# Identity products in TensorE's planned waits: a fused linear attention and SiLU layer on one core

## The chip, the cores and the metric

The kernel runs on one core of a Trainium2 chip. The metric is device time of one execution in microseconds (us), the median of several runs. The profile is one further execution, recorded by the hardware profiler; its times are told from the start of its span, and a line such as L830 is a line of the kernel's code.

## The reference

Two stages follow each other. The first is a block-wise linear attention with decay over 4 batches, 8 heads, 768 positions and 64 features per head; the second is a layer of 512 to 2048 to 512 features with SiLU between, over the 3072 tokens that the first yields.

```python
for b in range(nb):                      # blocks of 64 positions
    intra = einsum('bhic,bhjc->bhij', qb, kb) * Dmask
    intra = einsum('bhij,bhjd->bhid', intra, vb)
    inter = einsum('bhid,bhde->bhie', qb * lam_pow, kv_state)
    out[:, :, sl] = intra + inter
    kv_state = lam_block * kv_state + einsum('bhsd,bhse->bhde', kb * rev_pow, vb)
x = out.transpose(0, 2, 1, 3).reshape(B * S, H * D)
h = x @ w_in
return (h * sigmoid(h)) @ w_out
```

## The kernel before

The work is cut into units of 128 positions of one batch, 24 of them. Twelve sets of two units each carry the attention; the first four sets are the first 256 positions of one batch each ("paired", L414 to L556), the others are the same 128 positions of two batches.

Of a set, k, q and v are loaded by SyncE's queue (L349 for the first four sets, L351 after), 512 KB each. VectorE or ScalarE casts k and q to bf16 (`kq`, through the helper `copy`, L313 and L315). TensorE turns them with the identity into `tr` (L442), and they are copied back as `kqT`. VectorE scales v into `vd` (L320, the helper `tt`, where all its additions and products are recorded). TensorE then makes the state products `d_ps` (L463), the scores `st_ps` (L514), and, when VectorE has masked the scores, the outputs `x_ps` (L538 from the block itself, L543 from the carried state). VectorE makes the carried state of `d_ps` (the tiles `y`, `xf`), and ScalarE or GpSimd copies it into `xe` (L317 is GpSimd's copy). VectorE brings `x_ps` out as `xt`.

The layer's first product (`product1`, L830) takes 128 features of w_in at a time as the stationary operand; for the first four groups of units a quarter of w_in serves 16 products of 128x256, in two banks of PSUM. ScalarE applies SiLU (L839) into `g`. The second product is plain for the first eight units (L861, a bank per unit, four products to each quarter of w_out) and by a seven-product scheme of Strassen's kind for the others (L1072); the last group's first product uses such a scheme too (L944).

The weights are loaded and cast to bf16 by GpSimd's queue in quarters: L364 for w_in, L367 for w_out. Their order among the sets' loads is a string, `SEQUENCE = "s0 i0 s1 i1 i2 s2 i3 o0 s3 o1 o2 o3 s4"`. Where weights follow a set in it, GpSimd first copies one column of that set's k (`gate`, L331), so it waits for that load to land; all these GpSimd tasks stand in a chain (`prior`), and its copies of `xe` stand in the same instruction stream.

All other order comes from the class `Planner`. Each piece of work is a task with a key (its priority), the engines that may run it with a cost for each, the tasks that it depends on, and the buffers that it needs from pools of fixed size (8 banks of PSUM under "bank"). `order()` runs an event loop over planned time: at each event, an engine that is free takes the ready task of the lowest key whose buffers can be had; a buffer comes back to the end of its pool when the last task that uses it has its planned end; a task takes slots from the front. Loads are modelled as shares of the DMA engines. The list that comes out is the order in which the kernel then emits its instructions, on each engine, and each engine runs its own in that order. So planned times decide the order and the slots, and on the chip semaphores make each instruction wait for its data. TensorE may start at a planned 0.8 us (`BEGIN`).

The identity that the turns use is a constant, `ident` (L252 to L257), made by GpSimd early on.

Of the kernel before, what the change touches and what calls it, by code (L numbers as in the profile page):

```python
# [8 lines left out]
F32 = mybir.dt.float32  # L9
# [28 lines left out]
class Planner:  # L38

    LAT = {"PE": 0.23, "ACT": 0.06, "DVE": 0.06, "POOL": 0.08, "SP": 0.0}  # L40
    BEGIN = {"PE": 0.8, "ACT": 8.3, "DVE": 4.5, "POOL": 4.7, "SP": 0.8}
    FIRST, LAST, AHEAD = {"SP": 1.9, "ACT": 1.15, "POOL": 2.5}, 1.0, 0.75

    def __init__(self, pools):
        self.pools = {n: list(range(c)) for n, c in pools.items()}
        self.tasks = []

    def add(self, key, on, fn, deps=(), bufs=(), nbytes=0, kind=None, prior=(), late=0.0):
        key = key if isinstance(key, tuple) else (key,)
        t = Task(key, on, fn, deps, list(bufs) + [b.with_ for b in bufs if b.with_], nbytes, kind, prior, late)  # L50
        for b in t.bufs:
            b.left += 1
        self.tasks.append(t)
        return t

    def order(self):
        for i, t in enumerate(self.tasks):
            t.key = (t.key, i)
            t.left = len(t.deps) + len(t.prior)
            for d in t.deps:  # L60
                d.users.append(t)
            for d in t.prior:
                d.next.append(t)
        free = dict(self.BEGIN)
        waiting = {e: [] for e in free}
        ready = {e: [] for e in free}
        events, release, out = [], [], []
        started = set()
        queues = {e: [] for e in ("SP", "POOL", "ACT")}
        clock = [0.0]  # L70
        seq = 0

        def arm(t):
            for e in t.on:
                heapq.heappush(waiting[e], (t.ready, t.key, id(t), t))
            heapq.heappush(events, t.ready)

        def finish(t, e):
            nonlocal seq
            for b in t.bufs:  # L80
                b.left -= 1
                if not b.left:
                    seq += 1
                    heapq.heappush(release, (t.end, seq, b))
                    heapq.heappush(events, t.end)
            for u in t.users:
                u.left -= 1
                u.ready = max(u.ready, free[e] if e == "PE" and "PE" in u.on else t.end)
                if not u.left:
                    arm(u)  # L90

        def transfer(now):

            while True:
                at = clock[0]
                active = [(e, q[0]) for e, q in queues.items() if q and q[0][1] <= at + 1e-9]
                later = [q[0][1] for q in queues.values() if q and q[0][1] > at + 1e-9]
                cycle = max([sum(j[3][1] for _, j in active)] + [j[3][2] for _, j in active])
                speed = [16e-3 * j[3][0] / cycle for _, j in active]
                step = min([j[2] / v for (_, j), v in zip(active, speed)] + [x - at for x in later], default=None)  # L100
                if step is None or at + step > now + 1e-9:
                    if now > at:
                        for (_, j), v in zip(active, speed):
                            j[2] -= (now - at) * v
                        clock[0] = now
                    return None if step is None else at + step
                clock[0] = at + step
                for (e, j), v in zip(active, speed):
                    j[2] -= step * v
                    if j[2] <= 1e-9:  # L110
                        queues[e].pop(0)
                        j[0].end = clock[0] + self.LAST + j[0].late
                        finish(j[0], e)

        events += free.values()
        heapq.heapify(events)
        for t in self.tasks:
            if not t.left:
                arm(t)
        while len(out) < len(self.tasks):  # L120
            if not events:
                stuck = [t for t in self.tasks if id(t) not in started and not t.left]
                raise RuntimeError(f"plan stuck after {len(out)} of {len(self.tasks)}: "
                                   f"{[(t.key, list(t.on), [b.pool for b in t.bufs]) for t in stuck[:8]]}")
            now = heapq.heappop(events)
            after = transfer(now)
            while release and release[0][0] <= now:
                _, _, b = heapq.heappop(release)
                self.pools[b.pool].append(b.slot)
            for e in free:  # L130
                while waiting[e] and waiting[e][0][0] <= now:
                    _, key, i, t = heapq.heappop(waiting[e])
                    heapq.heappush(ready[e], (key, i, t))
                if free[e] > now:
                    continue
                if e == "SP" and sum(j[2] for j in queues[e]) > self.AHEAD:
                    continue
                kept, took, short = [], None, set()
                while ready[e]:
                    key, i, t = heapq.heappop(ready[e])  # L140
                    if i in started:
                        continue
                    need = {}
                    for b in t.bufs:
                        if b.slot is None:
                            need[b.pool] = need.get(b.pool, 0) + 1
                    lacks = {p for p, n in need.items() if len(self.pools[p]) < n}
                    if lacks or short & set(need):
                        short |= lacks
                        kept.append((key, i, t))  # L150
                        continue
                    mine = now + t.on[e]
                    if any(max(free[o], now) + d < mine - 1e-9 for o, d in t.on.items() if o != e):
                        kept.append((key, i, t))
                        continue
                    took = t
                    break
                for k in kept:
                    heapq.heappush(ready[e], k)
                if took is None:  # L160
                    continue
                t = took
                started.add(id(t))
                for b in t.bufs:
                    if b.slot is None:
                        b.slot = self.pools[b.pool].pop(0)
                free[e] = now + t.on[e]
                heapq.heappush(events, free[e])
                out.append((now, len(out), e, t))
                for u in t.next:  # L170
                    u.left -= 1
                    u.ready = max(u.ready, free[e])
                    if not u.left:
                        arm(u)
                if t.nbytes:
                    start = max(free[e] + self.FIRST[e], queues[e][-1][1] if queues[e] else 0.0)
                    queues[e].append([t, start, t.nbytes, t.kind])
                    after = transfer(now)
                else:
                    t.end = free[e] + self.LAT[e]  # L180
                    finish(t, e)
            if after is not None:
                heapq.heappush(events, max(after, now + 1e-6))
        transfer(now + 100.0)
        return out
# [3 lines left out]
def kernel(  # L189
# [10 lines left out]
    nc = tc.nc  # L200
# [29 lines left out]
    plan = Planner(POOLS)  # L230
    add = plan.add

    def tile_of(b, shape, dt, name):
        if b.tile is None:
            pool = ps if b.pool == "bank" else sb
            b.tile = pool.tile(shape, dt, tag=f"{b.pool}{b.slot}", name=name)
        return b.tile
# [4 lines left out]
        out=lam_sb,  # L242
# [7 lines left out]
    for t in xe_tiles:  # L250
        nc.vector.memset(t, 0.0)
    ident = const.tile([128, 128], BF16, name="ident")  # L252
    nc.gpsimd.memset(ident, 0.0)
    nc.gpsimd.affine_select(
        out=ident, in_=ident, compare_op=AL.not_equal, fill=1.0,
# [9 lines left out]
    for c, r in enumerate(halves):  # L265
        nc.gpsimd.affine_select(
            out=tri[r], in_=tri[r], compare_op=AL.is_ge, fill=0.0,
# [6 lines left out]
    for r in halves:  # L274
        nc.gpsimd.iota(iota_2[r], pattern=[[0, 1]], base=0, channel_multiplier=2)
        for a in range(2):
            for b in range(2):
                nc.gpsimd.affine_select(
                    out=tri_2[r, a, b], in_=tri_2[r, a, b], compare_op=AL.is_ge, fill=0.0,
# [511 lines left out]
    for si, o in enumerate(infos):  # L791
# [6 lines left out]
        else:  # L798
            if open_ is None:
                after_first(o, burst((o.s - 0.5, 0), [first_part(o)]))  # L800
            else:
                a, b = second_part(open_), first_part(o)
                t = burst((o.s - 0.5, 0), [a, b])
# [334 lines left out]
    for i in range(PLAIN, NU, 4):  # L1138
        product2(by_rank[i:i + 4])

    for _, _, e, t in plan.order():
        t.fn(e)

# [29 lines left out]
```

## Time and profile before

| What | Value |
|---|---|
| three runs | 206.91, 207.32, 209.9 us; median 207.32 |
| the profiled execution's own time | 207.82 us |
| its span, first to last instruction | 206.1 us |
| mean granted TensorE clock over the span | 0.989 |
| busy: TensorE, weight loads, VectorE, ScalarE, GpSimd | 187.0, 132.9, 134.8, 107.4, 52.4 us |
| moved by DMA | 33.92 MB, mean 165 GB/s |
| TensorE busy from 0 to 20 us | 9.66 us |
| TensorE busy from 20 to 25 us | 1.66 us |
| TensorE busy from 25 to 60 us | 34.79 us |

How to read it: the busy time of TensorE (PE) is that of overlapping matmuls whose ends are modelled, so it tells where the engine stood still rather than how well it ran. The granted clock is the share of full speed that the throttle let through. The chain that ended last is followed back from the last instruction, at each step to what released it; its shares say which engine's work made up the span. A landing is the time from a load's issue to its last byte.

### The profile page before, as it was taken

What the parts mean: (1) busy time and instruction counts of PE and PEld (TensorE: products, weight loads), DVE (VectorE), ACT (ScalarE), POOL (GpSimd) and SP (SyncE); (2) the same over time, 40 slices, a digit from 0 to 9 for tenths busy, and PEclk for the clock granted to TensorE, in tenths of its full rate; (3) what the DMA queues carried; (4) which work ended last, traced back from release to release, by engine and by line L of the source; (5) the groups of instructions that cost most, each with busy time, mean ns of one, the idle gap of its engine ahead of it and who ended that gap; (6) DMA issues with size and microseconds to landing.
All of it is one profiled execution on the core that took longest, in us unless ns stands there. A gap on an engine that the chain in (4) does not pass through costs nothing.

```text
span 206.1 us, 5719 instructions
## 1 busy us (share of the span) xinstructions
PE 187.0 (91%) x2445; PEld 132.9 (64%) x2464; DVE 134.8 (65%) x249; ACT 107.4 (52%) x195; POOL 52.4 (25%) x76
## 2 busy tenths in 40 slices
PE   0459399999999999999999999998999999999993
PEld 0347288786667565544578648474675778888882
DVE  6488632767950467716989953999758995665411
ACT  3637267874336453375734492745615453766420
POOL 7231400401130111222565013346003221222200
PEclk9999889999999999999999999999999999999999
DMA  3999999999999999999999999905101110102213
GB/s 99 292 253 260 228 222 265 235 199 214 228 238 249 156 216 231 238 219 195 263 213 234 203 213 240 244 7 117 39 3 54 51 54 0 54 0 102 88 52 118
DMA packets 88617, 33.92 MB, mean 165 GB/s; under 512 B 67088, under 2 KB 87568, under 8 KB 88592
## 3 DMA queue, kind: packets, MB, share of 16 engines
q1 hardware_dynamic: 79232, 23.60, 57.3%
q0 software_dynamic: 4224, 4.19, 12.2%
q10 hardware_dynamic: 5136, 5.77, 8.7%
q8 instruction: 19, 0.31, 0.7%
q14 instruction: 6, 0.05, 0.1%
HBM read 27.27 MB, written 6.29 MB: 163 GB/s over the span
## 4 chain that ended last, share of the span: by engine, by line
PE 82%; DMA 8%; DVE 7%; issue 1%; ACT 0%; POOL 0%; POOLq 0%; DVEq 0%
PE h_ps L830 31%; PE o_ps L1072 22%; PE o_ps L861 13%; PE h_ps L944 6%; DMA w_in_bf<-in_moe_w_in_dram 5%; DMA raw<-in_k_dram 3%; PE x_ps L687 2%; DVE s L320 2%; PE tr L442 2%; DVE g L320 1%; PE d_ps L647 1%; PE x_ps L679 1%; PE st_ps L657 1%; PE x_ps L538 1%; DVE kq L315 1%
## 5 line engine op out<-in xcount | busy, mean ns | idle before, releaser
L830 PE MATMUL h_ps<-xt,w_in_bf 128*128 128x256 bf16 (+1 forms) x439 | 75.7, 322 | 4.7 <-DMA w_in_bf<-in_moe_w_in_dram 3.3
L839 ACT ACTIVATE g<-h_ps 128x512 bf16<-128x512 f32 x80 | 47.1, 594 | 45.7 <-PE h_ps L830 45.0
L830 PEld LDWEIGHTS <-w_in_bf 128*128 128x128 bf16 x448 | 43.7, 99 | 30.1 <-DMA w_in_bf<-in_moe_w_in_dram 3.5
L861 PE MATMUL o_ps<-w_out_bf,g 128*128 128x512 bf16 x118 | 29.7, 379 | 0.6 <-issue 0.2
L320 POOL TENSOR_TENSOR s<-g,s 128x512 bf16<-128x512 bf16 x16 | 19.0, 1188 | 43.1 <-DVE s L320 26.8
L320 DVE TENSOR_TENSOR st<-st_ps,tri 128x512 bf16<-128x512 f32 x32 | 20.5, 681 | 11.2 <-PE st_ps L657 11.2
L1072 PEld LDWEIGHTS <-g 128*128 128x128 bf16 x256 | 24.9, 98 | 4.4 <-ACT g L839 0.3
L320 DVE TENSOR_TENSOR xt<-x_ps,lam_xe 128x512 bf16<-128x512 f32 x24 | 15.9, 699 | 15.2 <-PE x_ps L687 9.5
L1072 PEld LDWEIGHTS <-s 128*128 128x128 bf16 x192 | 18.7, 98 | 2.6
L861 PEld LDWEIGHTS <-g 128*128 128x128 bf16 x128 | 12.1, 98 | 12.0
L320 POOL TENSOR_TENSOR vd<-raw,lam_v 128x512 bf16<-128x512 f32 x10 | 13.3, 1334 | 25.1 <-DMA raw<-in_v_dram 19.7
L313 ACT ACTIVATE kq<-raw 128x512 bf16<-128x512 f32 x27 | 16.2, 621 | 2.1 <-DMA raw<-in_q_dram 1.6
L320 DVE TENSOR_TENSOR osb<-o_ps,m 128x512 f32<-128x512 f32 (+1 forms) x15 | 8.7, 583 | 10.9 <-ACT m L313 6.8
L1072 PE MATMUL o_ps<-wsum,g 128*128 128x256 bf16 x128 | 15.3, 272 | 0.0
L1072 PE MATMUL o_ps<-w_out_bf,s 128*128 128x256 bf16 x128 | 15.3, 273 | 0.0
L442 PE MATMUL tr<-ident,kq 128*128 128x128 bf16 x64 | 7.0, 260 | 8.8 <-POOL gate L331 6.9
L1072 PE MATMUL o_ps<-w_out_bf,g 128*128 128x256 bf16 x128 | 15.0, 273 | 0.0
L320 DVE TENSOR_TENSOR s<-g 128x512 bf16<-128x512 bf16 x16 | 8.2, 510 | 10.4 <-ACT g L839 6.6
L313 ACT ACTIVATE m<-o_ps 128x512 f32<-128x512 f32 (+1 forms) x14 | 7.0, 503 | 11.4 <-PE o_ps L1072 11.4
L320 DVE TENSOR_TENSOR vd<-raw,lam_v 128x512 bf16<-128x512 f32 x14 | 9.2, 681 | 5.0 <-DMA raw<-in_v_dram 5.0
L313 ACT ACTIVATE osb<-o_ps 128x512 f32<-128x512 f32 (+1 forms) x12 | 6.7, 562 | 10.4 <-PE o_ps L861 6.5
L315 DVE CAST kq<-raw 128x512 bf16<-128x512 f32 x21 | 9.1, 451 | 3.8 <-DMA raw<-in_k_dram 2.0
(88 smaller groups left out, 215.1 us busy)
## 6 DMA issues: line engine op xcount, KB each, us to landing
raw<-in_k_dram SPq DMA_DIRECT2D x12, 512.0 KB, 8.2
raw<-in_q_dram SPq DMA_DIRECT2D x12, 512.0 KB, 8.5
raw<-in_v_dram SPq DMA_DIRECT2D x12, 512.0 KB, 8.0
out_dram<-osb ACTq DMA_DIRECT2D x20, 256.0 KB, 3.6
w_in_bf<-in_moe_w_in_dram POOLq DMA_DIRECT2D x4, 512.0 KB, 10.0
w_out_bf<-in_moe_w_out_dram POOLq DMA_DIRECT2D x4, 512.0 KB, 11.7
out_dram<-osb ACTq DMA_DIRECT2D x4, 128.0 KB, 1.7
out_dram<-osb SPq DMA_DIRECT2D x4, 128.0 KB, 1.7
```

Of the source, the lines that this page charges most:

```text
L313: nc.scalar.activation(o, i, AF.Copy)
L315: nc.vector.tensor_copy(o, i)
L320: (nc.vector if e == "DVE" else nc.gpsimd).tensor_tensor(o, a, b, op=op)
L442: nc.tensor.transpose(t[:, m, a], o.kq_of()[:, i, m, a], ident)
L538: nc.tensor.matmul(t[rh, m], lhsT=o.vd_of()[r, 2 * m + h, a, :], rhs=o.st_of(h)[r, m, a], start=m == 0 and a == 0, stop=True, skip_group_c ...
L647: nc.tensor.matmul(d_of(c)[rp, j, m, :], lhsT=o.kq_of()[r, j, 0, m, p, :], rhs=o.vd_of()[r, j, 2 * m + p, :], start=j == 0 and m == 0, sto ...
L687: nc.tensor.matmul(x_of(c)[:, j, m, :], lhsT=o.xe[c].tile[:, (bs[0] + j) % 2, m, :], rhs=o.kqT_of()[:, j, 1, m, halves[c]], start=False, s ...
L830: nc.tensor.matmul(t[:, j, :], lhsT=w_in_bf[:, ko, 128 * (m1 + j):128 * (m1 + j) + 128], rhs=xt[gi].tile[:, ko, :], start=(ko == 0), stop= ...
L839: nc.scalar.activation(t[:, half * per:half * per + per], bank.tile, AF.Silu)
L861: nc.tensor.matmul(t, lhsT=g.tile[:, j, 128 * gp:128 * gp + 128], rhs=w_out_bf[:, ko, :], start=(ko == 0), stop=(ko == KO - 1))
L944: nc.tensor.matmul(t[:, j, :], lhsT=W[w]()[:, k2, f:f + 128], rhs=X(r)[:, k2, :], start=first and j == 0 and k2 == 0, stop=True, skip_grou ...
L1072: nc.tensor.matmul(t[:, i_, :], lhsT=src(j)[:, k2, 128 * r:128 * r + 128], rhs=W[w]()[:, 2 * j + k2, :], start=first and i_ == 0 and j == ...
```

## The change

The planner gets a filler. In its event loop, where TensorE is free and no task can be started, between a planned 1.7 and 30 us and with more than two banks free, it takes the bank that came back last, books TensorE for 0.44 us (before 6 us) or 0.22 us (after), gives the bank back at the end of that time, and puts the filler into the list. A filler issues four matmuls of the identity with itself, 128x128 each, into the four quarters of the bank. Nothing reads what they write.

```diff
+    WARM, COLD = (1.7, 30.0), 6.0
...
+        self.filler = None
...
-        while len(out) < len(self.tasks):
+        fillers = 0
+        while len(out) < len(self.tasks) + fillers:
...
                 if took is None:
+
+                    if e == "PE" and self.filler and self.WARM[0] <= now < self.WARM[1] and len(self.pools["bank"]) > 2:
+                        b = Buf("bank")
+                        b.slot = self.pools["bank"].pop()
+                        free[e] = now + (0.44 if now < self.COLD else 0.22)
+                        seq += 1
+                        heapq.heappush(release, (free[e], seq, b))
+                        heapq.heappush(events, free[e])
+                        out.append((now, len(out), e, self.filler(b)))
+                        fillers += 1
                     continue
...
+    def filler(b):
+        def go(e):
+            t = tile_of(b, [128, 4, 128], F32, "ones")
+            for i in range(4):
+                nc.tensor.matmul(t[:, i, :], lhsT=ident, rhs=ident, start=i == 0, stop=True, skip_group_check=True)
+
+        return Task("filler", {"PE": 0.22}, go, [], [])
+
+    plan.filler = filler
     for _, _, e, t in plan.order():
         t.fn(e)
```

## The prediction

> **What bounds the kernel now.** I read the page first: its 40 slices and the shares of the chain that ended last.
>
> ```profile
> span 206.1 us, 5719 instructions
> ...
> PE   0459399999999999999999999998999999999993
> ...
> PEclk9999889999999999999999999999999999999999
> DMA  3999999999999999999999999905101110102213
> ...
> PE 82%; DMA 8%; DVE 7%; issue 1%; ACT 0%; POOL 0%; POOLq 0%; DVEq 0%
> ```
>
> TensorE is full from the sixth slice to the last. Its holes are all in the first 24 us, and the granted clock dips in slices five and six, right behind the last hole. The DMA engines are full from the second slice to the 26th (about 134 us), so in that time loads land when bytes allow, not when somebody asks earlier. The waits of TensorE by the view of waits are, from 5 to 30 us, 6.9, 3.3, 1.3, 0.9, 0.9 and 0.2 us; from 30 us on they are this and 0.2 us of issue:
>
> ```profile
> PE h_ps L830 <- DVE xt L320: 0.7, 1, 0.7
> ```
>
> Next the chain in order of time (start, length, what), for the place of the hole:
>
> ```profile
> 9.40 0.94 PE tr L442 x7
> ...
> 13.59 0.12 POOL gate L331
> 13.71 10.23 DMA w_in_bf<-in_moe_w_in_dram
> ...
> 23.99 3.41 PE h_ps L830 x16
> ...
> 28.87 1.75 PE h_ps L830 x16
> ```
>
> The second quarter of w_in is issued at 13.71 and lands at 23.94. The first 16 products on it take 3.41 us, where 16 of the same shape take 1.75 us at 28.87: 1.66 us lost. Busy time by stretch, cut so that each has one clock (columns: length, then busy time and count of PE, PEld, DVE, ACT, POOL, then granted clock, DMA share, GB/s):
>
> ```profile
> 10.57:13.98 3.41, 1.71 (x64) 1.33 (x63) 2.83 (x6) 1.55 (x4) 0.78 (x3) 1.00 1.19 219
> 13.98:17.40 3.42, 3.15 (x50) 2.57 (x51) 3.39 (x8) 1.77 (x4) 1.76 (x3) 1.00 1.15 308
> 17.40:20.81 3.41, 3.03 (x85) 2.38 (x82) 2.43 (x6) 2.60 (x6) 0.00 (x0) 1.00 1.21 237
> 20.81:24.22 3.41, 0.23 (x3) 0.21 (x3) 3.11 (x6) 1.45 (x3) 2.15 (x5) 1.00 1.19 217
> 24.22:27.64 3.42, 3.42 (x28) 2.26 (x29) 0.00 (x0) 1.10 (x3) 0.26 (x1) 0.50 1.18 242
> ```
>
> After a stretch with 0.23 us of work the clock is 0.50 for 3.42 us. The column shows 1.00 before 17.4 too, but the durations there are those of a halved clock: eight transposes take 0.94 us at 7.28 and 9.40, and 0.45 us at 28.42. So TensorE is slow until about 17.4, fast, and slow once more from 24.22 to 27.64.
>
> Last, what stands behind that loss: loads that TensorE meets just after they land.
>
> ```profile
> 28.70 1.47 PE L830 MATMUL h_ps<-xt,w_in_bf 128*128 128x256 bf16 x12
> ...
> 37.10 0.45 PE L463 MATMUL d_ps<-vd,kq 64*64 64x64 bf16 x32
> ...
> 51.36 3.62 PE L861 MATMUL o_ps<-w_out_bf,g 128*128 128x512 bf16 x15
> ```
> ```profile
> 35.24 1.29 DVE L320 TENSOR_TENSOR vd<-raw,lam_v 128x512 bf16<-128x512 f32 x2 [3.72 <-DMA raw<-in_v_dram]
> ```
> ```profile
> DMA to landing us min/median/max: 7.8/10.0/13.2
> ```
> ```profile
> DMA to landing us min/median/max: 8.0/11.7/13.3
> ```
>
> The third quarter of w_in (issued 14.46, 13.2 us to land, the first of the two landing lines) is there at 27.7 and first used at 28.70: 1.0 us of slack. VectorE waits 3.72 us for the third set's v, starts its two products at the landing (35.24) and ends at 36.53; the state products that need them start at 37.10: 0.57 us of slack. The last quarter of w_out (third of the issues that start at 37.40, so 38.9, plus 13.3) lands at 52.1; TensorE comes to it after eight products of 0.216 us from 51.36, at 53.09: 1.0 us of slack.
>
> **The change part by part.** It takes nothing away. It adds fillers: wherever the planner finds TensorE with nothing to start between 1.7 and 30 us of its own time, it books 0.44 us (0.22 from 6 us on) and a free bank, and issues four 128x128 products of the identity.
>
> How many: the planner's own list for the unchanged code, gone through by hand of its rules, leaves TensorE unoccupied for 5.6 us up to the first transposes, then 1.6, 2.1, 2.6, 0.9, 1.7 and 0.5 us. That is 10 + 5 fillers before the first transposes, then 7 + 9 + 12 + 4 + 8 + 2 = 42, 57 in all, 228 products. From the trace alone: 12 us idle between 1.7 and 30 give about 45.
>
> What one takes: four products of the transposes' shape, by their rows 0.45/8 x 4 = 0.225 us at full clock and 0.94/8 x 4 = 0.47 us at half. So the booked 0.22 fits the full clock only.
>
> (a) The first 15 start once the identity is made (GpSimd's select on it ends at 1.37) and fill up to between 6.5 us (clock up after 3.4 us) and 1.4 + 15 x 0.47 = 8.5 us (never up). The transposes' data is ready at 7.24. I take their start at 7.4 and the clock up by then, since 3.15 us of work in 3.42 brought it up at 17.4: -0.49 us for the transposes, +0.15 for the fillers. Bounds: -0.5 to +1.2 us.
>
> (b) The next 16 hold TensorE until about 9.4 and 11.8 us, near where the real products start now (9.40, 12.04). The v of the first set lands at about 10.0 by its median of 8.0 us from 1.93, so VectorE's two products (1.28 us, now at 10.70) can start 0.5 us sooner and the states at 11.8. GpSimd's copy at 13.14, its gate at 13.59 and the load at 13.71 hang on that chain. Queued behind the copy on GpSimd are both the second and the third quarter of w_in. I take 0.3 us sooner (bounds 0.7 sooner, 0.5 later), so w_in's second quarter at 23.6.
>
> (c) The 12 that follow the scores run to about 15.5; the transposes that now run from 14.02 to 15.47 are queued behind them, and the x products (now 15.39) wait for VectorE's masks until about 15.2. Late by 0.3 to 0.5 us, repaid by 0.46 us from the transposes and 0.5 us from the x products at full clock: nothing net. With the clock still halved this cover is gone, and it costs 12 x 0.25 = 3.0 us.
>
> (d) The 8 in the hole at 20.65 take 1.8 us. Each writes a bank that VectorE must have read (its copy ends at 20.77), so they start there and end at about 22.6, a microsecond short of the load. The stretch then holds 1.8 + 0.4 us of work in place of 0.23. The nearest rows: 0.23 of 3.41 lost the clock, 3.03 of 3.41 kept it; 1.71 of 3.41 did not win it. Unknown between; I take kept (2.2 is nearer to 3.03 than to 0.23). Worth 1.66 us if kept, 0 if not.
>
> (e) The last two, 0.45 us, stand ahead of the third quarter's products. With (b) and (d), TensorE would come to these at 28.70 - 0.3 - 1.66 + 0.45 = 27.2 and the load lands at 27.4: 1.3 us sooner than now.
>
> (f) What is late next: the states at 37.10 would be reached at 35.8, and v still lands at 35.2, because the DMA engines are full. The second half waits for VectorE until 36.6, so they end near 36.85 in place of 37.5: 0.6 us is left of 1.3. The w_out quarter's 1.0 us of slack then covers it, and later waits are nothing. PSUM: a filler takes a bank only where more than two are free, so a real task loses at most one filler's 0.22 us, counted above.
>
> Sum against the profiled execution (207.82 us, span 206.1): 207.82 - 0.6 = 207.2. The three runs have their median 0.5 us below it, 207.32, so 206.7 for the median.
>
> [...]
>
> **The rivals.**
> No gain reaches the end: the clock is lost in (d) all the same, or the median run had not lost it, or the fillers of (a) and (c) give back what it saves. For it: slack of only 0.57 us at 37.10, 0.5 us between the profiled execution and the median. Against: 1.66 us is three times that slack. 207.1 to 208.3 us; centre 207.4.
> All of it reaches the end: the DMA order shifts so that v and the w_out quarters land sooner as well. For it: half of w_in is issued sooner. Against: DMA share 1.15 to 1.21 throughout, nothing idle to use. 1.66 + 0.3 gives 205.4, bounds 204.8 to 206.2.
> Slower: identity products do not raise the clock. Then 40 fillers up to 24 us take 0.25 us more than booked, 10 us; the hole takes 1.5 of it, so TensorE comes to the second quarter 8 us late: about 215. From 17 such fillers (17 x 0.25 = 4.2 us) it decides the sign past the bound. Against: the transposes, also against the identity, were part of the 3.15 us that raised it at 17.4.
> The plan comes out in another order: fillers shift planned starts by up to 0.2 us, and choices between ScalarE and VectorE follow. A microsecond or two either way; the 0.7 us wait at 140.6 on VectorE shows one place where it would count.
>
> **How the numbers follow.** Forecast (206.2 to 207.1) 0.55; no gain 0.22; all of it 0.12; another order, 205 to 209, 0.06; slower 0.05. The predicted time is the first's, 206.7. The range 205.4 to 208.4 takes in the first two, half of the third, and most of the fourth. Two per cent, 4.1 us, is about what a measurement of this kernel can tell from no change: past it lies the slower rival, 0.05, and on the fast side hardly anything, 0.02, since the whole loss at the clock is 1.66 us. Within it 0.93.
>
> **What would show it.** Right: about 225 more products with the identity before 30 us; eight transposes in 0.45 us from the first set on; 16 products in 1.75 us behind w_in's second quarter and no 0.50 in the clock between 20 and 30 us; then a new wait of TensorE on VectorE's vd near 36, and v landing at 35 as before. Wrong: transposes starting past 8 us (a), the gate's load issued later than 13.7 (b), x products past 16 us (c), the clock at 0.50 again (d), or no new wait at 36 and a time below 206 (f).

## The result and the profile after

The changed kernel takes 218.09 us (median of 6, 217.69 to 218.24) against 207.27 us for the kernel before beside it; the ratio of the mean times is 1.050, with a 95% interval from 1.0445 to 1.0551. A few executions take longer (of the kernel before up to 215.0 us, and one of booked_right 333 us), and they stand outside the ratios and the counts below. The forecast was 206.7 us, with 0.05 on a kernel slower by over 2%. The profiled execution took 218.16 us, 10.3 us more than that of before.

From the page of the changed kernel, the same rows as those shown of before:

```profile
span 216.4 us, 6181 instructions
...
PE   6998999999999999999999999998999999999993
...
PEclk9999999999999999999999999999999999999999
DMA  3999999999913999999999999890601110102213
...
PE 91%; DVE 5%; issue 2%; ACT 0%; POOL 0%; POOLq 0%; DVEq 0%
```

The holes of TensorE are filled and the clock's dip is gone, as the change says. But the whole span is 10 us longer, and the DMA engines, full before, now have a hole of their own in slices 12 and 13. TensorE's waits (us in total, times, longest), all that the view of waits lists:

```profile
PE ones L1158 <- POOL ident L267: 1.4, 1, 1.4
PE h_ps L843 <- DVE xt L333: 0.7, 1, 0.7
PE o_ps L874 <- issue: 0.2, 1, 0.2
```

No wait on another engine has taken the place of the old ones: from 1.44 us on, TensorE hardly waits for any of them. So the 10 us are in what stands in its own queue. The chain in order of time (start, length, what) shows it:

```profile
2.10 0.60 PE ones L1158 x4
2.74 0.60 PE ones L1158 x4
...
10.42 0.58 PE ones L1158 x4
11.00 0.85 PE tr L455 x8
...
15.81 0.40 PE ones L1158 x4
16.20 0.04 issue
16.25 0.40 PE ones L1158 x4
...
19.71 0.40 PE d_ps L476 x30
```

`ones` is a filler's tile. Fillers start 0.64 us apart at half clock and 0.44 us apart at full clock; the plan booked 0.44 and 0.22. Of the 0.44, the four products begin within 0.17 us, the last needs 0.22 us more to its end, and 0.04 to 0.06 us pass before the next filler begins. Between eight transposes there is no such stop. TensorE's weight loads, which the view of waits lists apart, show the stops as waits of about 0.2 us each, 9.6 us in 50 of them:

```profile
PEld L1158 <- issue: 9.6, 50, 0.2
```

What is waited for stands in the trace's semaphores (the counters by which one instruction tells another that it is done). 50 of the 58 fillers follow another filler directly. The first product of each of these waits for a semaphore that TensorE alone raises, and the instruction that raised it last is the last product of the filler before.

The first transposes, whose data is there at 7.3 us, start at 10.8 in place of 6.95 (by the timeline), and the first state products at 19.6 in place of 11.4. GpSimd's gate and the loads of w_in's second and third quarters hang on these (timeline of GpSimd after):

```profile
21.23 0.18 POOL L344 COPY gate<-raw 128x1 f32<-128x1 f32 x1
21.35 1.50 POOL L377 DMA_DIRECT2D w_in_bf<-in_moe_w_in_dram  x2
```

The loads start at 21.35, 7.6 us later than the 13.71 of before.

The sum over the whole of TensorE: there are 58 fillers (the forecast said 57), and the time from the start of each of their products to the next start on TensorE adds up to 27.7 us; they were booked 10 x 0.44 + 48 x 0.22 = 15.0 us. They filled 13.5 us of waits of before. The fillers and the first wait of 1.4 us, less the old waits, are 27.7 + 1.4 - 13.5 = 15.6 us, and 10.3 came out at the end. The other 5.3 us was saved by the real work: its products, counted in the same way and without the waits, take 182.6 us in place of 187.8, since less of them runs at half clock (the 16 products behind w_in's second quarter: 1.75 us in place of 3.41).

### The profile page after: what moved, and what is told of

Its sections match the earlier page's. It is cut to its first block, busy times and chain, and to the rows that moved or that the text cites. A ratio compares the mean times of both kernels' runs of the same rounds, so it can differ in the third digit from the quotient of the medians.

```text
span 216.4 us, 6181 instructions
## 1 busy us (share of the span) xinstructions
PE 206.5 (95%) x2677; PEld 148.3 (69%) x2696; DVE 132.8 (61%) x247; ACT 107.9 (50%) x195; POOL 51.6 (24%) x78
## 4 chain that ended last, share of the span: by engine, by line
PE 91%; DVE 5%; issue 2%; ACT 0%; POOL 0%; POOLq 0%; DVEq 0%
PE h_ps L843 30%; PE o_ps L1085 21%; PE o_ps L874 13%; PE ones L1158 12%; PE h_ps L957 6%; PE x_ps L700 2%; PE tr L455 2%; DVE s L333 2%; DVE g L333 1%; PE d_ps L660 1%; PE x_ps L551 1%; PE x_ps L692 1%; PE st_ps L670 1%; PE d_ps L476 1%; DVE y L333 1%
## 5 line engine op out<-in xcount | busy, mean ns | idle before, releaser
L843 PE MATMUL h_ps<-xt,w_in_bf 128*128 128x256 bf16 (+1 forms) x439 | 74.7, 317 | 1.2 <-DVE xt L333 0.7
L843 PEld LDWEIGHTS <-w_in_bf 128*128 128x128 bf16 x448 | 43.0, 98 | 25.8 <-DVE xt L333 1.0
L1158 PE MATMUL ones<-ident 128*128 128x128 bf16 x232 | 26.1, 245 | 4.5 <-POOL ident L267 1.4
L1158 PEld LDWEIGHTS <-ident 128*128 128x128 bf16 x232 | 18.3, 110 | 11.5 <-issue 9.6
L333 POOL TENSOR_TENSOR vd<-raw,lam_v 128x512 bf16<-128x512 f32 x10 | 11.4, 1140 | 25.9 <-DMA raw<-in_v_dram 25.8
L326 ACT ACTIVATE kq<-raw 128x512 bf16<-128x512 f32 x28 | 17.0, 621 | 0.5 <-DVE osb L333 0.4
L326 ACT ACTIVATE kqT<-tr 128x512 bf16<-128x512 bf16 x8 | 4.6, 589 | 12.5 <-DVE kqT L328 7.2
```

The costliest lines, as they stand in the source:

```text
L326: nc.scalar.activation(o, i, AF.Copy)
L333: (nc.vector if e == "DVE" else nc.gpsimd).tensor_tensor(o, a, b, op=op)
L843: nc.tensor.matmul(t[:, j, :], lhsT=w_in_bf[:, ko, 128 * (m1 + j):128 * (m1 + j) + 128], rhs=xt[gi].tile[:, ko, :], start=(ko == 0), stop= ...
L1158: nc.tensor.matmul(t[:, i, :], lhsT=ident, rhs=ident, start=i == 0, stop=True, skip_group_check=True)
```

## The experiments

Three theories stood at first. W: a filler that takes a bank writes a new tile there, so it waits until the products of the filler before, in the same bank, have come to their end (have drained). M: four products of that kind take that long by themselves. O: the planner's order of tasks, which the booked fillers change, costs the time. Times are medians; ratios are of mean times to the kernel before on the same chip, with 95% intervals. The name behind each heading is that of the run.

**The plan without the products** (plan_only).

```diff
 def go(e):
-    t = tile_of(b, [128, 4, 128], F32, "ones")
-    for i in range(4):
-        nc.tensor.matmul(t[:, i, :], lhsT=ident, rhs=ident, ...)
+    pass
```

> The planner books all 58 fillers as in the change, but nothing is issued for them: the order and the slots are those of the change, the products are left out. Theory W (each filler waits until the products of the one before have drained, because it writes the same bank as a new tile, so it takes 0.64 us at half clock and 0.44 us at full clock where 0.44 and 0.22 are booked): the time of before, 206.5 to 208. Theory M (four such products with their weight loads take that long by themselves): the same, 206.5 to 208. Theory O (the other order of tasks and the other banks cost the time): 214 or more.

Measured: 208.1 us, ratio 1.0044 (1.0017 to 1.007). The order is not where the 5% are: O falls as their cause. A cost of 0.4% is left, which lies with the order and the slots or what follows from them; the interval, 0.2 to 0.7%, excludes that it is nothing.

**The same tile again** (one_tile).

```diff
+    ones = {}
...
 def tile_of(b, shape, dt, name):
     if b.tile is None:
         pool = ps if b.pool == "bank" else sb
+        if name == "ones" and b.slot in ones:
+            b.tile = ones[b.slot]
+            return b.tile
         b.tile = pool.tile(shape, dt, tag=f"{b.pool}{b.slot}", name=name)
+        if b.pool == "bank":
+            ones.pop(b.slot, None)
+            if name == "ones":
+                ones[b.slot] = b.tile
     return b.tile
```

> All 58 fillers are issued, but a filler that takes a bank whose last user was a filler writes the same tile again, so it needs no wait for itself. Theory W: a filler takes 0.43 us at half clock and 0.22 us at full clock, the first transposes start between 7.2 and 8.0 us, the load of w_in's second quarter is issued near 13.7, time 206 to 208. Theory M: fillers stay at 0.64 and 0.44 us and the time at 217 to 219. Theory O: 214 or more. The part of the prediction on the clock: no stretch at half clock between 20 and 30 us, 206.7.

Measured: 208.69 us, ratio 1.0082 (1.0046 to 1.0119). All 232 products are still there. Timeline of TensorE:

```profile
1.44 5.60 PE L1166 MATMUL ones<-ident 128*128 128x128 bf16 x60 [1.44 <-POOL ident L275]
6.99 0.90 PE L463 MATMUL tr<-ident,kq 128*128 128x128 bf16 x8
...
12.96 2.62 PE L1166 MATMUL ones<-ident 128*128 128x128 bf16 x44
...
25.42 0.64 PE L559 MATMUL x_ps<-st,vd 64*64 64x128 bf16 x31
27.17 0.21 PE L559 MATMUL x_ps<-st,vd 64*64 64x128 bf16 x1 [1.11 <-issue]
```

Eleven fillers (44 products) take 2.62 us with the drain of the last, 0.22 us each; in the change they were 0.44. The transposes start at 6.99 and the second quarter's load at 13.63. The 50 waits of the weight loads in the change are down to one:

```profile
PEld L1166 <- issue: 0.5, 1, 0.5
```

M falls: the same products without the wait cost what was booked. Taking the wait away brings back some nine of the eleven us. The time misses W's range all the same: 1.4 us over the kernel before are left, which W did not expect. In the profiled execution 1.1 us of idle time stands in the last line of the timeline above, a stop of TensorE that the last section comes back to.

**Twice the waits** (split).

```diff
-t = tile_of(b, [128, 4, 128], F32, "ones")
-for i in range(4):
+for h in range(2):
+    c = Buf("bank")
+    c.slot = b.slot
+    t = tile_of(c, [128, 4, 128], F32, "ones")
+    for i in (2 * h, 2 * h + 1):
         ...
```

> As the change, but each filler's four products go to two tiles of the same bank, two each, so there are twice as many waits for the filler's own products and as many products as before. Theory W: 0.33 x 2 = 0.66 us for a filler at full clock and 0.48 x 2 = 0.96 at half, so 58 fillers take 13 to 17 us more than in the change: 229 to 236. Theory M (the products themselves take the time): 218.

Measured, in two executions: 239.59 us, ratio 1.155 (1.1479 to 1.1613). M's 218 us is excluded. The direction is W's, but the time is past its range: the chain of this run has the half fillers 0.43 us apart far past the place where the clock rose in the change.

```profile
16.61 0.39 PE ones L1161 x2
16.99 0.04 issue
17.04 0.39 PE ones L1161 x2
```

That is 0.85 us for a filler, where W had 0.66 us at full clock: two products in each 0.43 us did not bring the clock up, and its first rise in the trace is at 50.5 us. The miss is in the clock, not in the wait.

**Booked as long as they take** (booked_right).

```diff
-    WARM, COLD = (1.7, 30.0), 6.0
+    WARM, COLD = (1.7, 30.0), 14.0
...
-                        free[e] = now + (0.44 if now < self.COLD else 0.22)
+                        free[e] = now + (0.64 if now < self.COLD else 0.44)
```

> The fillers keep their tiles and their waits, but the planner books 0.64 us before a planned 14 us and 0.44 us after, so there are 27 of them. Theories W and M: TensorE comes to its real work about as in the plan, first transposes near 8 us, 206.5 to 208.5. Theory O, in which fillers do harm by moving the order: 212 or more. A fourth way, that any product of the identity slows the loads by its reads: 212 or more as well, with a lower rate of DMA.

Measured: 207.6 us, ratio 1.0012 (0.9984 to 1.0041). With its waits left in, a filler does no harm when the plan knows its length: there are then 27, which end when the real work comes due (first transposes at 7.01). This run has half as many products as the change, so by itself it does not show that the products do nothing to the loads; one_tile, with all 232 of them, does to within its 1.4 us. Together they put the loss down to the waits, times their number, in a queue that runs in order.

**Only ahead of the first transposes** (early_only).

```diff
-    WARM, COLD = (1.7, 30.0), 6.0
+    WARM, COLD = (1.7, 6.0), 6.0
```

> Fillers only up to a planned 6 us: 10 of them, with their tiles and waits. Theories W and M: 10 x 0.64 = 6.4 us from 1.44, so the first transposes start at 7.9 in place of 7.28, and w_in's second quarter is issued 0.3 to 0.7 us later than 13.71; 207.3 to 208.5. Theory O: 212 or more, since the booked time already moves the order. If the fillers raise the clock before the transposes, these take 0.45 us and the delay is repaid: 207.0.

Measured: 209.25 us, ratio 1.0085 (1.0054 to 1.0116), somewhat above the range of W. The ten fillers take 6.4 us and the transposes start at 7.60, 0.65 us late, at half clock (eight in 0.9 us): ten fillers with waits do not raise it. The load of w_in's second quarter starts at 14.16, 0.45 us late, as expected. The trace has two further waits of TensorE on VectorE, of 0.6 and 0.8 us near 105 and 111 us, that before does not have; whether they come of the order or of the delay was not told apart.

**One wide product in place of four** (wide_one). It starts from one_tile; the order in which the tiles `xe` are set to zero is turned round, so that the one that the fillers read is there first.

```diff
-t = tile_of(b, [128, 4, 128], F32, "ones")
-for i in range(4):
-    nc.tensor.matmul(t[:, i, :], lhsT=ident, rhs=ident, ...)
+t = tile_of(b, [128, 512], F32, "ones")
+nc.tensor.matmul(t, lhsT=ident, rhs=xe_tiles[-1][:, 0].rearrange("p m e -> p (m e)"), ...)
...
-    for t in xe_tiles:
+    for t in xe_tiles[::-1]:
```

> As one_tile, but a filler is one product of the identity with 512 columns of zeros in place of four of 128 columns: the same 0.22 and 0.43 us, a quarter of the instructions. It asks what is left of one_tile's 1.4 us over the kernel before. Theory F: in one_tile TensorE stood still for 1.3 us at 25.84 with nothing to wait for, at its 961st instruction, 512 instructions after a like stop in booked_right and 2048 ahead of one in plan_only, because its code had not been fetched; with 348 instructions fewer the stop goes or is short, and the time is 206.3 to 207.6. Theory O: the planner's other order costs it; the time is that of plan_only, 207.8 to 208.5.

Measured: 207.62 us, ratio 1.0008 (0.9975 to 1.0041). The median is just past F's range and under O's, and the stop on issue is gone from the trace (0.2 us, as in the change, is all that is left under that name). The interval lies under one_tile's, but the trace has new short waits on ScalarE (1.1 us) in the stop's place, and one execution cannot tell how often the stop comes. So F's time fits, nearly, and its cause is not shown (last section).

**Only the hole in front of w_in's second quarter** (hole_only), the part of the prediction that carried its gain; the tile is kept as in the second experiment.

```diff
-    WARM, COLD = (1.7, 30.0), 6.0
+    WARM, COLD = (20.0, 24.0), 6.0
```

> Fillers without the wait for themselves (one_tile's way) only between a planned 20 and 24 us: nine of them, and the order of all tasks is that of the kernel before. It tests the sum of the prediction by itself. If the clock is kept and the loads' slack lets 0.6 us through: ratio 0.997. If an execution of the kernel before mostly doesn't lose the clock there, or the loads give it all back: ratio 0.999 to 1.002. If the clock falls all the same: 1.000 with a stretch of half clock in the profile.

Measured: 207.02 us, ratio 0.9972 (0.9946 to 0.9998). Busy time by stretch (columns as in the prediction), then the timeline of TensorE:

```profile
20.81:24.22 3.41, 2.25 (x46) 2.02 (x35) 3.38 (x7) 1.46 (x3) 2.04 (x4) 1.00 1.19 217
24.22:27.64 3.42, 3.10 (x60) 2.48 (x58) 1.08 (x3) 1.75 (x4) 0.40 (x1) 1.00 1.18 251
```
```profile
21.12 1.95 PE L1166 MATMUL ones<-ident 128*128 128x128 bf16 x32 [0.17 <-DVE y L341]
24.06 1.92 PE L851 MATMUL h_ps<-xt,w_in_bf 128*128 128x256 bf16 x16 [0.99 <-DMA w_in_bf<-in_moe_w_in_dram]
...
36.19 0.32 PE L484 MATMUL d_ps<-vd,kq 64*64 64x64 bf16 x16
36.69 0.32 PE L484 MATMUL d_ps<-vd,kq 64*64 64x64 bf16 x16 [0.18 <-DVE vd L341]
```

With 2.25 us of busy time in 3.41 the clock is kept, the 16 products behind the load take 1.9 us with the end of the last, and TensorE comes to the state products at 36.2 and waits there for vd, where before it came at 37.1 and did not wait.

**Two variants of it**, one with the wide product (hole_wide) and one with the change's own fillers and their waits (hole_waits).

> As hole_only, but each of the nine fillers is one product of the identity with 512 columns of zeros: 18 instructions in place of 72. It is the best guess from the runs so far, and a second test that the work in the hole is worth something. If what it does is to keep the clock: ratio 0.995 to 0.999, like hole_only's 0.9972. If hole_only's gain was chance: 0.999 to 1.002. If zeros do not count as work for the clock: a stretch of half clock behind the hole, 1.000.

Measured: 207.17 us, ratio 0.9985 (0.996 to 1.001).

> The change's own fillers, with their waits, only between a planned 20 and 24 us: nine of them. Theory W: 0.44 us each, so one delays the state products by 0.2 us and eight take 3.5 us from 20.8 on, up to 24.3, 0.3 us past the landing of w_in's second quarter. The clock is kept or not by products that fill about half of each 0.44 us; in the change it stayed at full with them. Kept: ratio 0.997 to 1.001. Lost: 1.001 to 1.004. Theory M gives no other time here.

Measured: 207.41 us, ratio 0.9996 (0.9971 to 1.0021). Its eight fillers run from 21.9 to 25.2 with full clock after them (the 16 products behind them take 1.91 us). All three are at or under the time of before, and only the first has an interval that excludes it, narrowly. None is a version of which a gain over before is certain; all three beat the changed kernel by 5%. That fillers there keep the clock is shown better than by the times: none of the 35 executions of the three has a mean granted clock under 0.996, while a quarter of those of before have 0.992 or less (counted below).

## Why the prediction was wrong, point by point

What one filler takes is the step that failed. The prediction worked it out as four products of the transposes' row, 0.225 us at full clock and 0.47 at half, "so the booked 0.22 fits the full clock only". The row is of eight products into one tile. A filler is four products into a tile of its own in a bank whose last user is a filler too, and it waits for that one's end. The measured size is 0.44 and 0.64 us; with the tile kept (one_tile) it is 0.22 and 0.43. Beside the identity in (a), the only thing that the prediction lets a filler wait for is VectorE's read of its bank, in (d); a wait for the filler before it is nowhere in the sum, and no reason is given for leaving it out.

The slower rival came near with about 215 us and the second quarter 8 us late (measured 218.1 and 7.6), but for a wrong reason, and that is luck. It took products of the identity not to raise the clock, and 40 fillers to be 0.25 us too long for it. Even by its own terms the sum is too high: the first ten are booked at 0.44 us, so 0.47 us makes them only 0.03 us too long, and its 10 us would be 7.8. What was measured is 27.7 - 15.0 = 12.7 us over 58 fillers, 0.22 us on average, from another cause. The products of the identity do raise the clock: without the waits (one_tile) it is up at 5.8 us. In the changed kernel, with the same products spaced by their waits, it was up at 14.08 us.

(a) The prediction took the transposes at 7.4 and the clock up by then. They started at 10.8, and the trace has the clock up at 14.08; the bound of 1.2 us late was missed. Without the waits the transposes start at 6.99 and the clock is up at 5.8, as forecast. The reason given, that 3.15 us of busy time in 3.42 had raised the clock, was not sound: 3.13 us in 3.41 did not raise it in the changed kernel (last section).

(b) The second quarter's load was forecast 0.3 us sooner and came 7.6 us later. Without the waits it is at 13.63 against 13.71, hardly sooner either: the gain there was put too high.

(c) Nothing net was forecast, and 3.0 us if the clock was still halved. The clock was up by then, and the eleven fillers behind the scores took 4.8 us for a booked 2.4 all the same, by the waits.

(d) That about 2.2 us of work would keep the clock was right: 2.25 us did in hole_only.

(e), (f) The new wait on vd near 36, which takes back part of the gain, is there in hole_only (0.18 us, the second half at 36.7). The 0.6 us that it leaves was expected as 0.997 and measured as 0.9972, but the interval reaches from 0.02% to 0.54%, and the two variants lie at 0.9985 and 0.9996.

How often the clock is lost: of 68 executions of before beside these runs, 17 have a mean granted clock of 0.992 or less, like the 0.989 of the profiled one, and 51 have 0.996 or more. Their medians are 207.95 and 207.35 us. The mean does not tell where the clock was lost, and in kernels with other fillers it is lost at times too (3 of 9 executions of booked_right); that none of the 35 executions of the three kernels with fillers in the hole alone lost it points at the hole. By the means, the same program lost the clock in one execution of four.

So the loss is worth 0.6 us at the end and not 1.66, and the median of before mostly does not contain it; the prediction, whose first rival names this ("the median run had not lost it"), still took the whole 0.6 us off the median. By this the median has little to gain from the hole. Why hole_only shows as much as 0.28% stays open: on its chip even the executions of before that kept the clock have a median of 207.52 us, 0.5 us above its 207.02. Chance within its interval is enough.

The order of tasks cost 0.4% by plan_only; the prediction gave it a rival of its own, a microsecond or two either way, and no price in the sum.

## What to carry to other kernels

The cost of an added instruction can be its spacing among its own kind and not its length: look for what each must wait for, its own forerunner included, before a row of back-to-back instructions is taken for it. Here the 58 fillers with a tile each held TensorE for 27.7 us, and the same fillers with their tile kept for 15.8. Work that is to fill a wait in a queue that runs in order must be booked at its true length, or end early: 27 fillers booked at what they took were harmless, 58 that took nearly twice their booking cost 5%. Before a stall is filled, follow its time to the end: here the whole loss at the clock was worth 0.6 us behind the next loads, and in a quarter of the executions only.

## What the runs showed of the hardware

In the changed kernel a TensorE that looks busy did not raise the clock. By the records it is busy for 3.13 of 3.41 us in this stretch, at half clock throughout:

```profile
7.26:10.67 3.41, 3.13 (x23) 2.31 (x23) 0.04 (x1) 1.85 (x2) 0.91 (x1) 1.00 1.13 280
```

The records overlap (a filler's product stands there for 0.31 us at half clock, and the next starts 0.107 us after it), so the starts tell more. In this stretch four products of 0.107 us start in each 0.64 us, two thirds of the time. With eight transposes back to back in the next 3.4 us the clock rose, at 14.08. In split, with two products in each 0.43 us between the real work, it had not risen by 50 us. Fillers without waits (one_tile) raised it at 5.8 us.

The traces of before and of the change, counted by starts: for each product, take 0.107 us per 128 columns at half clock and half of that at full clock as the time in which it streams, count products side by side once, and cut the time into stretches of 3.41 us (the length of the halved one in before), backwards and forwards from the first rise. In the changed kernel the four stretches ahead of the rise at 14.08 have products streaming for 0.45, 0.57, 0.62 (the line above) and 0.75 of their time; in before the three ahead of the rise at 17.40 have 0.45, 0.39 and 0.79. In the changed kernel the clock then stayed up through every stretch, the lowest with 0.47 (20.9 to 24.3, with the fillers that fill half of each 0.44 us), and fell to 0.50 at 215.5, behind one with 0.19. In before it fell at 24.22, behind the hole with 0.06, rose at 27.64, behind the halved stretch with 0.93, and fell at 205.1, behind one with 0.19. At full clock neither trace has a stretch between 0.19 and 0.47, so what such a stretch does is not shown. Some records are missing, so the shares are near values, and they are those of two executions.

A stop without a wait: in one_tile TensorE stands still for 1.3 us after 961 of its instructions, in booked_right for 0.7 us after 449, and in plan_only for 0.6 us after 3009; the differences are 512 and 2048. The queue of instruction loads has 21 packets of 16 KB in the changed kernel (the line below), for 2677 products and 2696 weight loads of TensorE: one for about 256 of them. Before it has 19 for 4909, one for 258.

```profile
q8 instruction: 21, 0.34, 0.7%
```

By these counts alone it is a guess that the stops have to do with the loading of code; that 348 instructions fewer (wide_one) took the stop away fits it. But the packets do not show code that comes late: the one before the stop of one_tile had ended at 25.6 us, 0.26 us ahead of it, those before the other two stops 1.0 and 0.8 us ahead, and none came in during a stop. The cause stays open; no run tested it directly.
